# Sliding-window attention and a two-layer block: one transpose for a query block's two blocks of keys

## The chip, the cores and the metric

The kernel runs on one core of a Trainium2 chip. The metric is the device time in microseconds; the kernel before was timed in three runs, and the profile is of one further execution. The engines are TensorE (PE; its weight loads are listed as PEld), VectorE (DVE), ScalarE (ACT), GpSimd (POOL) and SyncE (SP), whose queue issues the loads and stores.

## What is computed

```python
def _attn_ref(q, k, v, n_sink, window):          # q, k, v: 4 x 8 x 768 x 64, n_sink 4, window 128
    scores = np.matmul(q, k.transpose(0, 1, 3, 2)) / np.sqrt(D)
    rel = pos[:, None] - pos[None, :]
    keep = (pos[None, :] < n_sink) | ((rel >= 0) & (rel < window))
    scores = np.where(keep, scores, -1e9)
    a = np.exp(scores - np.max(scores, axis=-1, keepdims=True))
    a = a / (np.sum(a, axis=-1, keepdims=True) + 1e-09)
    return np.matmul(a, v)

x = attn_out.transpose(0, 2, 1, 3).reshape(3072, 512)
h = x @ w_in                                     # 512 x 2048
out = (h * np.cos(h)) @ w_out                    # 2048 x 512
```

## The kernel before

The sequence of a batch is cut into six blocks of 128 rows. A *chunk* is two blocks of queries of one batch (`CB = 2`), so there are 12 chunks of 8 heads each. Since the window is 128 keys, a query block needs its own block of keys (the *diagonal* block), the block before it (*prev*) and the first keys of the batch (the *sinks*, of which 8 columns are carried). A row of probabilities for query block j lies in tile `p` as 264 columns: 128 of prev, 8 sinks, 128 of diag. The first query block of a batch has no prev.

The first three chunks (24 heads, "early") run while the weights are still unpacked; they use a shorter method in plain fp32 (`scores_pe`, `p_out`, `values_pe`). The other nine chunks use splits into two fp32r parts, hi and lo, whose products give nearly fp32: `q_hi`/`q_lo`, `k_hi`/`k_lo`, `v_hi`/`v_lo`, and for the probabilities `p_hi`/`p_lo`. Eight of these nine have a first block that is not block 0 of its batch.

A head of those eight chunks goes through these steps: scores on PE (L885); masking with the row's minimum on DVE (L898); exp with row sums on ACT (L907), four heads together; the reciprocal of the sums on DVE (L916, L917); normalization of each row block on DVE, POOL or ACT (`norm`, L925 and L927, tile `p`); four transposes on PE (`turn`, L997, tile `tp`: prev and diag for each of two query blocks); the fp32r cast of the turned probabilities on ACT (`p_hi`, L1006, tile `phi`) and the remainder on DVE (`p_lo`, L1013, tile `plo`); seven value matmuls on PE (`values`, L1051, tile `av`, with the sinks through `gt` and `vs`); a copy of the lower half on ACT (`x_low`, L1058, tile `xb`) and the sum on DVE (`x_sum`, L1065). `phi` and `plo` have one buffer each. Two heads fill 128 rows of the chunk's x; when eight heads are done the dense layers follow for that chunk in eight slots: `h` (L416), cosine and gate (L425 to L461), `acc` (L476).

Dense work of one chunk stands between the attention steps of the next. What sets the order is a planner (`Plan`): each step has the engines that may take it with an assumed duration, what it waits for, and a priority worked out from the offsets in table `C`. `order()` plays this through and hands out a fixed sequence for each engine, which the engines then follow in order; steps with several engines are placed there too. Steps marked `port=True` on DVE are not planned at the same time as POOL's. 160 filling matmuls (`idle`, L1320) go in at the start where PE would have nothing.

The two transposes for each query block are issued by

```python
c0 = 0 if (kb == i - 1 or i == 0) else o.sw
nc.tensor.transpose(out=o.tp[:, n * P : (n + 1) * P], in_=o.p[:, i - o.i0, c0 : c0 + P], identity=ident)
```

Of the kernel before, what the change touches and what calls it, by code (L numbers as in the profile page):

```python
# [16 lines left out]
P = 128  # L17
# [23 lines left out]
def f32(ap):  # L41
    return ap.bitcast(F32)
# [127 lines left out]
def attn_moe_kernel(ctx, tc, q, k, v, n_sink, window, w_in, w_out, out):  # L170
# [485 lines left out]
    def banded_path():  # L656
# [7 lines left out]
        masks = m0, ma, mb = mk[:, :P], mk[:, P : 3 * P], mk[:, 3 * P :]  # L664
        diag, prev, cols = mb[:, SW:], mb[:, :P], ma[:, :P]
        vs = env.vs = ap.tile([P, H // GQ, GQ, 2, D], F32R, name="vs")
        env.kz = ap.tile([P, 2, NT], F32, name="kz", tag="plo")
        env.warm = ps.tile([P, P], F32, name="warm", tag="b0")

        def masked(m):  # L670
# [20 lines left out]
        for a, (b, i0) in enumerate(chunks):  # L691
            for h in range(H):
                o = Rec()
                o.a, o.b, o.i0, o.h, o.pair, o.odd = a, b, i0, h, h // 2, h % 2
                o.kb0 = max(i0 - 1, 0)
                o.nkb = i0 + CB - o.kb0
                o.sj = [j for j in range(CB) if i0 + j >= 2]
                o.cols = [
                    (kb, [i for i in (kb, kb + 1) if i0 <= i < i0 + CB]) for kb in range(o.kb0, o.kb0 + o.nkb)
                ]  # L700
                o.offs = [sum(len(c[1]) for c in o.cols[:n]) for n in range(len(o.cols) + 1)]
                o.n = o.offs[-1]
                o.sw = P if i0 == 0 else SW
                o.w = [P if i0 + j == 0 else o.sw + P for j in range(CB)]
                o.s_ps = {}
                o.tag = f"{b}_{i0}_{h}"
                heads.append(o)
# [126 lines left out]

        def p_out(o):
            def fn(e):
                o.pt = ap.tile([P, 4 * P], F32, name=f"pt_{o.tag}", tag="phi")
                copy(e, o.pt[:, : o.n * P], o.tp[:, : o.n * P])
            return fn

# [63 lines left out]
        def expo(o, j):  # L904
# [5 lines left out]
                )  # L910
            return fn

        def denom(o):
            def fn(e):
                n = o.nq
                nc.vector.tensor_single_scalar(out=o.st[:, 2, :n], in_=o.st[:, 1, :n], scalar=1.0e-9, op=ALU.add)  # L916
                nc.vector.reciprocal(out=o.st[:, 3, :n], in_=o.st[:, 2, :n])  # L917
            return fn

        def norm(o, j):  # L920
            def fn(e):
                w = o.w[j]
                r = o.lead.st[:, 3, o.nth, j : j + 1]
                if e is nc.scalar:
                    e.activation(out=o.p[:, j, :w], in_=o.p[:, j, :w], func=AF.Copy, scale=r)  # L925
                else:
                    e.tensor_scalar(  # L927
                        out=o.p[:, j, :w], in0=o.p[:, j, :w], scalar1=r, scalar2=1.0, op0=ALU.mult, op1=ALU.mult
                    )
            return fn  # L930
# [59 lines left out]
        def turn(o):  # L990
            def fn(e):
                o.tp = ps.tile([P, 4 * P], F32, name=f"tp_{o.tag}", tag=o.tp_bank)
                n = 0
                for kb, qs in o.cols:
                    for i in qs:
                        c0 = 0 if (kb == i - 1 or i == 0) else o.sw
                        nc.tensor.transpose(  # L997
                            out=o.tp[:, n * P : (n + 1) * P], in_=o.p[:, i - o.i0, c0 : c0 + P], identity=ident
                        )
                        n += 1  # L1000
            return fn

        def p_hi(o):
            def fn(e):
                o.phi = ap.tile([P, 4 * P], F32R, name=f"phi_{o.tag}", tag="phi")
                nc.scalar.copy(out=o.phi[:, : o.n * P], in_=o.tp[:, : o.n * P])  # L1006
            return fn

        def p_lo(o):
            def fn(e):  # L1010
                w = o.n * P
                o.plo = ap.tile([P, 4 * P], F32R, name=f"plo_{o.tag}", tag="plo")
                nc.vector.tensor_tensor(out=o.plo[:, :w], in0=o.tp[:, :w], in1=f32(o.phi)[:, :w], op=ALU.subtract)  # L1013
            return fn

        def values_pe(o, x):
# [179 lines left out]
        def softmax(group):  # L1196
            lead = group[0][1]
            T, DX, NM = (C["TQ"], C["XE"], C["NE"]) if lead.early else (C["T"], C["DX"], C["NM"])
            t = head_time(group[0][0]) - (len(group) - 4) * T - T + 3.9 + DX
            ready = [i for _, o in group for i in o.msk]  # L1200
            ex = [
                add(
                    [("ACT", act(o.w[j]) + 0.19)], expo(o, j), ready, t + 1.02 * n + 0.01 * j, table="exp"
                )
                for n, (_, o) in enumerate(group) for j in range(CB)
            ]
            t += 1.02 * (len(group) - 1) + 0.5
            d = add([("DVE", 0.35)], denom(lead), ex, t)
            for n, (_, o) in enumerate(group):
                o.nm = [  # L1210
                    add(
                        [("POOL", 0.2 + o.w[j] / 1200), ("DVE", dve(o.w[j], True, True)), ("ACT", act(o.w[j]))], norm(o, j), [d],
                        t + NM * n + 0.01 * j, port=True
                    )
                    for j in range(CB)
                ]
                lead.bst.users += o.nm

        def after_softmax(g, o):
# [49 lines left out]
                o.sinks = [o.first.vt, e3]  # L1269
            pt, bhi, blo = buf("tp", 1), buf("phi", 1), buf("plo", 1)  # L1270
            bav = buf("av", 1)
            p0 = add([("PE", 0.107 * o.n)], turn(o), o.nm + [pt], t + DA + 1.3)
            o.bp.users.append(p0)
            p1 = add([("ACT", act(o.n * P, False))], p_hi(o), [p0, bhi], t + DA + 1.8)
            p2 = add([("DVE", dve(o.n * P))], p_lo(o), [p1, blo], t + DA + 2.3)
            pt.users += [p1, p2]
            deps = [p2, v1, bav]
            if o.sj:
                oe = heads[g - o.h % GQ]
                deps += oe.sinks  # L1280
# [251 lines left out]
```

## Time and profile before

| | |
|---|---|
| median of three runs | 752.69 us (750.21 to 754.62) |
| the profiled execution | 750.97 us, its span 749.2 us |
| PE busy | 736.5 us, 98% of the span |
| DVE busy | 625.7 us, 84% |
| ACT busy | 560.7 us, 75% |
| POOL busy | 59.4 us, 8% |
| TensorE clock granted | 0.999 of full speed |

The span runs from the first to the last instruction of the program; the execution's time has 1.8 us more around it. Busy time is the union of an engine's instructions, so overlapping ones count once. Matmuls overlap: a matmul of 256 columns is listed with 0.28 us but the next one starts 0.12 us later, so the step from start to start is what one more or less of them is worth. Idle time of an engine that does not set the end costs nothing. Spans on POOL are rough.

### The profile page before, as it was taken

Reading aid. Unit: us, or ns where it says so; the run is one execution under the profiler, and the core shown is the slowest. Engines: PE = TensorE matmul, PEld = TensorE weight load, DVE = VectorE, ACT = ScalarE, POOL = GpSimd, SP = SyncE. Lnnn points to the kernel's source line nnn. Section 1 sums busy time; section 2 is a strip of 40 time slices with the busy share of each in tenths; the row PEclk is TensorE's granted clock in tenths of the full one; section 3 lists DMA queues with packets and bytes.
Section 4 is the critical chain, followed back from the end, with each engine's and each line's share of the span. In section 5 each row is a group of like instructions: output and inputs, shape, how many; then the busy total and the mean of one; then the engine's idle time right before and its main releaser. Section 6 shows DMA issues by size and latency. Waiting matters only on the chain.

```text
span 749.2 us, 15109 instructions
## 1 busy us (share of the span) xinstructions
PE 736.5 (98%) x4949; PEld 657.3 (88%) x4949; DVE 625.7 (84%) x1698; ACT 560.7 (75%) x1327; POOL 59.4 (8%) x137
## 2 busy tenths in 40 slices
PE   9999999999999999999999999999999999999996
PEld 8787766899899998898999999999999999999995
DVE  6998999768899998989999998998888988865331
ACT  4989778676978878678788688888688788774332
POOL 1000000000101110111110010100011111000000
PEclk9999999999999999999999999999999999999999
DMA  5755575222446546446464433232242333110000
GB/s 156 200 178 180 155 197 144 57 46 40 108 109 160 121 101 154 106 106 188 98 168 120 111 96 61 51 70 41 46 84 47 53 77 59 21 40 7 19 11 32
DMA packets 215608, 71.49 MB, mean 95 GB/s; under 512 B 204256, under 2 KB 204256, under 8 KB 215520
## 3 DMA queue, kind: packets, MB, share of 16 engines
q1 hardware_dynamic: 215232, 70.43, 38.8%
q8 instruction: 41, 0.67, 0.4%
q14 instruction: 47, 0.39, 0.2%
q10 hardware_dynamic: 288, 0.00, 0.0%
HBM read 64.10 MB, written 6.29 MB: 94 GB/s over the span
## 4 chain that ended last, share of the span: by engine, by line
PE 82%; DVE 11%; ACT 3%; DMA 2%; issue 1%; SPq 0%; POOL 0%; DVEq 0%; ACTq 0%; POOLq 0%
PE h L416 33%; PE acc L476 31%; PE av L1051 5%; PE s L885 4%; PE tp L997 4%; PE idle L1320 1%; DVE w_out L530 1%; DVE p L898 1%; DVE w_out L536 1%; PE acc L471 1%; DVE p L927 1%; DVE w_in L530 1%; DVE lo_in L566 1%; PE av L1027 1%; DVE lo_out L566 1%
## 5 line engine op out<-in xcount | busy, mean ns | idle before, releaser
L416 PE MATMUL h<-xhi,hi_in 128*128 128x256 f32 x768 | 222.8, 290 | 1.0 <-ACT pt L404 0.6
L416 PE MATMUL h<-xlo,hi_in 128*128 128x256 f32 x768 | 216.9, 282 | 0.0
L416 PE MATMUL h<-xhi,lo_in 128*128 128x256 f32 x768 | 216.7, 282 | 0.0
L416 PEld LDWEIGHTS h<-xhi,hi_in 128*128 128x128 f32 x768 | 146.1, 190 | 5.1 <-DVE glo L461 1.0
L416 PEld LDWEIGHTS h<-xhi,lo_in 128*128 128x128 f32 x768 | 146.2, 190 | 3.3 <-issue 0.5
L416 PEld LDWEIGHTS h<-xlo,hi_in 128*128 128x128 f32 x768 | 146.1, 190 | 0.0
L476 PE MATMUL acc<-hi_out,ghi 128*128 128x512 f32 x352 | 143.4, 407 | 0.4 <-DVE raw L406 0.4
L476 PE MATMUL acc<-hi_out,glo 128*128 128x512 f32 x352 | 138.4, 393 | 0.0
L476 PE MATMUL acc<-lo_out,ghi 128*128 128x512 f32 x352 | 138.3, 393 | 0.0
L425 ACT ACTIVATE yt<-h 128x512 int32<-128x512 f32 x96 | 57.2, 596 | 59.1 <-PE h L416 56.9
L898 DVE CUSTOM_DVE_ANT_0 p<-s,mk 128x264 f32<-128x264 f32 (+1 forms) x192 | 75.5, 400 | 23.0 <-PE s L885 18.9
L431 DVE SCALAR_TENSOR_TENSOR r<-h,yt 128x512 f32<-128x512 f32 x96 | 65.5, 682 | 34.4 <-ACT yt L425 34.0
L907 ACT ACTIVATE p<-p,st 128x264 f32<-128x264 f32 (+1 forms) x192 | 93.6, 489 | 0.5
L476 PEld LDWEIGHTS acc<-hi_out,glo 128*128 128x128 f32 x352 | 66.1, 188 | 15.0
L438 ACT ACTIVATE r<-r,neg 128x512 f32<-128x512 f32 x96 | 69.1, 723 | 9.7 <-DVE r L431 9.1
L476 PEld LDWEIGHTS acc<-hi_out,ghi 128*128 128x128 f32 x352 | 66.4, 189 | 7.7 <-DVE raw L406 0.6
L476 PEld LDWEIGHTS acc<-lo_out,ghi 128*128 128x128 f32 x352 | 66.6, 189 | 6.6
L461 DVE TENSOR_TENSOR glo<-h,ghi 128x512 fp32r<-128x512 f32 x88 | 60.1, 683 | 10.0 <-ACT ghi L455 9.9
L443 DVE TENSOR_TENSOR h<-h,r 128x512 f32<-128x512 f32 x88 | 60.2, 686 | 2.8 <-ACT r L438 2.7
L455 ACT CAST ghi<-h 128x512 fp32r<-128x512 f32 x88 | 51.3, 583 | 14.9 <-PE acc L476 14.2
L885 PE MATMUL s<-r,l 128*128 128x264 f32 (+2 forms) x288 | 59.3, 286 | 0.4 <-ACT vr L935 0.2
L885 PEld LDWEIGHTS s<-r,l 128*128 128x128 f32 x288 | 48.8, 189 | 7.9 <-DVE st L898 0.9
(128 smaller groups left out, 1328.1 us busy)
## 6 DMA issues: line engine op xcount, KB each, us to landing
raw<-in_moe_w_in_dram SPq DMA_DIRECT2D x32, 512.0 KB
raw<-in_moe_w_out_dram SPq DMA_DIRECT2D x32, 512.0 KB
xk<-in_k_dram SPq DMA_DIRECT2D x256, 48.0 KB
out_dram<-raw SPq DMA_DIRECT2D x24, 256.0 KB
v<-in_v_dram SPq DMA_DIRECT2D x64, 96.0 KB
xq<-in_q_dram SPq DMA_DIRECT2D x144, 32.0 KB
v<-in_v_dram SPq DMA_DIRECT2D x32, 64.0 KB
xq<-in_q_dram SPq DMA_DIRECT2D x24, 64.0 KB
```

Source lines behind the costliest of these rows:

```text
L416: nc.tensor.matmul(out=o.h[:, t, :], lhsT=w[:, fs], rhs=xx[:, c, :], start=(c == 0 and n == 0), stop=(c == NC - 1 and n == 2),)
L425: nc.scalar.activation(out=yt, in_=o.h, func=AF.Copy, scale=INV2PI, bias=0.25)
L431: nc.vector.scalar_tensor_tensor(out=o.r, in0=o.h, scalar=INV2PI, in1=yt, op0=ALU.mult, op1=ALU.subtract)
L438: nc.scalar.activation(out=o.r, in_=o.r, func=AF.Sin, scale=TWOPI_DOWN, bias=quarter)
L443: nc.vector.tensor_tensor(out=o.h, in0=o.h, in1=o.r, op=ALU.mult)
L455: nc.scalar.copy(out=o.ghi, in_=o.h)
L461: e.tensor_tensor(out=o.glo, in0=o.h, in1=f32(o.ghi), op=ALU.subtract)
L476: nc.tensor.matmul(out=x.acc[j], lhsT=gg[:, t, j * P : (j + 1) * P], rhs=w, start=(f == 0 and n == 0), stop=(f == NFT - 1 and n == 2),)
L885: nc.tensor.matmul(out=o.s_ps[j][:, :w], lhsT=o.l[:, j * P : (j + 1) * P], rhs=r.rearrange("p n s -> p (n s)")[:, c0 : c0 + w], start=(n = ...
L898: nc.vector.tensor_tensor_reduce(out=o.p[:, j, :w], in0=o.s_ps[j][:, :w], in1=masks[min(o.i0 + j, 2)][:, :w], op0=ALU.add, op1=ALU.min, sc ...
L907: nc.scalar.activation(out=o.p[:, j, :w], in_=o.p[:, j, :w], func=AF.Exp, bias=o.lead.st[:, 0, o.nth, j : j + 1], scale=-1.0, accum_out=o. ...
L1051: nc.tensor.matmul(out=dst, lhsT=lhs, rhs=rhs, start=(n == 0), stop=(n == len(seq) - 1), skip_group_check=True)
```

## The change

In the eight chunks without a block 0 (64 heads, `o.one`), a row of prev is nonzero only right of the row's own position and a row of diag only up to it, since the window is as long as a block: the two never overlap. After exp, a new step `lap` on DVE or POOL adds the 128 columns of diag onto the 128 of prev, for both query blocks in one instruction of 128x2x128; normalization then covers 136 columns (`o.nw`) instead of 264; `turn` makes two transposes instead of four; `p_hi` and `p_lo` handle 256 columns instead of 512. The two blocks are parted after the turn by two selections on POOL (`part`, `affine_select`), which take hi and lo together (128x4x128 each): the first writes the diag half, the second overwrites the sum with its prev half. `phi` and `plo` become the two halves of one lasting tile `pz` with one buffer, so `p_hi` waits for both to be free. The value matmuls read `pz` as they read `phi` and `plo`. The kz and pt tiles of the early heads share that memory (`firsts`). The numbers of table `C` are new almost throughout.

```diff
+                o.one = i0 > 0
+                o.nw = [SW] * CB if o.one else o.w
...
+        def lap(o):
+            def fn(e):
+                e.tensor_tensor(out=o.p[:, :, :P], in0=o.p[:, :, :P], in1=o.p[:, :, SW:], op=ALU.add)
+            return fn
...
         def norm(o, j):
             def fn(e):
-                w = o.w[j]
+                w = o.nw[j]
...
-                for kb, qs in o.cols:
+                for j in range(CB if o.one else 0):
+                    nc.tensor.transpose(out=o.tp[:, j * P : (j + 1) * P], in_=o.p[:, j, :P], identity=ident)
+                for kb, qs in o.cols if not o.one else ():
...
+                if o.one:
+                    nc.scalar.copy(out=env.pz4[:, 0, :, 0], in_=o.tp[:, :NT].rearrange("p (j r) -> p j r", j=CB))
+                else:
+                    nc.scalar.copy(out=o.phi[:, : o.n * P], in_=o.tp[:, : o.n * P])
...
+                if o.one:
+                    nc.vector.tensor_tensor(
+                        out=env.pz4[:, 1, :, 0], in0=o.tp[:, :NT].rearrange("p (j r) -> p j r", j=CB),
+                        in1=f32(env.pz4)[:, 0, :, 0], op=ALU.subtract,
+                    )
...
+        def part(n):
+            def fn(e):
+                sign = (-1, 1)[n]
+                nc.gpsimd.affine_select(
+                    out=env.pz4[:, :, :, n], in_=f32(env.pz4)[:, :, :, 0], pattern=[[0, 2], [0, CB], [sign, P]],
+                    compare_op=ALU.is_ge, fill=0.0, base=n - 1, channel_multiplier=-sign,
+                )
+            return fn
...
+            laps = [
+                [add(sub(NT), lap(o), ex[CB * n : CB * n + CB], t + 1.02 * n + 0.3 + C["LP"], port=True)] if o.one else []
...
-            p1 = add([("ACT", act(o.n * P, False))], p_hi(o), [p0, bhi], t + DA + 1.8)
-            p2 = add([("DVE", dve(o.n * P))], p_lo(o), [p1, blo], t + DA + 2.3)
+            p1 = add([("ACT", act(n * P, False))], p_hi(o), [p0, bhi, blo], t + DA + 1.8)
+            p2 = add([("DVE", dve(n * P))], p_lo(o), [p1], t + DA + 2.3)
             pt.users += [p1, p2]
-            deps = [p2, v1, bav]
+            if o.one:
+                p1 = add([("POOL", 0.18 + 2 * NT / 1200)], part(1), [p1, p2], t + DA + 2.7)
+                p2 = add([("POOL", 0.18 + 2 * NT / 1200)], part(0), [p1], t + DA + 3.2)
+            deps = [p1, p2, v1, bav]
...
-    "T": 6.142, ...  "DA": 0.079, "DV": 5.203, ...
+    "T": 7.838, ...  "DA": 0.108, "DV": 3.174, ...
```

What the new order makes of this is seen at three places. In the names, `_3_2_3` is batch 3, first block 2, head 3; the last number is the buffer's. First PE, around the values of head 2 and the turn of head 3 in batch 3, before:

```order
L885 MATMUL s_3_2_7_0_8303<-r2_3_2_7_8292,l_3_2_7_8244 128x264
L1051 MATMUL av_3_2_2_8308<-phi_3_2_2_8279,vr_3_2_2_8286 128x256
L1051 MATMUL av_3_2_2_8308<-gt_77,vs_94 128x256
L1051 MATMUL av_3_2_2_8308<-phi_3_2_2_8279,vr_3_2_2_8286 128x128
L1051 MATMUL av_3_2_2_8308<-plo_3_2_2_8299,vr_3_2_2_8286 64x128
L1051 MATMUL av_3_2_2_8308<-plo_3_2_2_8299,vr_3_2_2_8286 64x256
L1051 MATMUL av_3_2_2_8308<-phi_3_2_2_8279,vr_3_2_2_8286 128x128
L1051 MATMUL av_3_2_2_8308<-plo_3_2_2_8299,vr_3_2_2_8286 64x128
L997 MATMUL tp_3_2_3_8319<-ident_76,p_3_2_3_7877 128x128 x4
```

and PE at the same place now:

```order
L1003 MATMUL tp_3_2_3_8261<-ident_76,p_3_2_3_7782 128x128 x2
L416 MATMUL h_75_8226<-xhi_9_7360,hi_in_4_462 128x256
L416 MATMUL h_75_8226<-xhi_9_7360,lo_in_4_503 128x256
L416 MATMUL h_75_8226<-xlo_9_7376,hi_in_4_462 128x256
L416 MATMUL h_75_8226<-xhi_9_7360,hi_in_5_513 128x256
L416 MATMUL h_75_8226<-xhi_9_7360,lo_in_5_527 128x256
L416 MATMUL h_75_8226<-xlo_9_7376,hi_in_5_513 128x256
L1083 MATMUL av_3_2_2_8275<-pz_2099,vr_3_2_2_8188 128x256
```

The turn of the next head, two transposes instead of four, has moved from behind the values of this head to a place ahead of them, with dense work between.

On POOL, in batch 1 while its blocks 2 and 3 are worked on, before (`tk`: sink columns copied into K; `p`: normalization; `vr`: remainder of v):

```order
L406 COPY tk_1_2_5_3741<-ts_1_2_0_3162 128x3x8
L927 TENSOR_SCALAR p_1_2_1_3456<-p_1_2_1_3456,st_1_2_0_3326 128x264
L927 TENSOR_SCALAR p_1_2_2_3550<-p_1_2_2_3550,st_1_2_0_3326 128x264
L940 TENSOR_TENSOR vr_1_2_1_3979<-v32_74,vr_1_2_1_3979 128x3x64
L406 COPY tk_1_2_7_4031<-ts_1_2_0_3162 128x3x8
L940 TENSOR_TENSOR vr_1_2_2_4053<-v32_74,vr_1_2_2_4053 128x3x64
L940 TENSOR_TENSOR vr_1_2_3_4113<-v32_74,vr_1_2_3_4113 128x3x64
```

and POOL there now:

```order
L1042 AFFINE_SELECT pz_2099<-pz_2099 128x4x128 x8
L406 COPY tk_1_2_5_3739<-ts_1_2_0_3160 128x3x8
L935 TENSOR_SCALAR p_1_2_1_3412<-p_1_2_1_3412,st_1_2_0_3313 128x136
L935 TENSOR_SCALAR p_1_2_2_3536<-p_1_2_2_3536,st_1_2_0_3313 128x136
L406 COPY tk_1_2_6_3839<-ts_1_2_0_3160 128x3x8
L1042 AFFINE_SELECT pz_2099<-pz_2099 128x4x128 x8
```

Eight selections stand for four heads; the remainders of v have left POOL here. In the whole program POOL has 128 selections, 38 normalizations (before 55), 6 remainders of v (before 35) and 19 sink copies (before 35). Of the 192 normalizations DVE now has 56 (before 81) and ACT 98 (before 56); of the remainders of v DVE has 66 (before 37).

On DVE, at the end of batch 1, around the remainder of the probabilities of head 3 of its last chunk, before:

```order
L1065 TENSOR_TENSOR x_6_1_4977<-av_1_4_2_4926,xb_75 64x256
L443 TENSOR_TENSOR h_42_4820<-h_42_4820,r_42_4934 128x512
L898 ISA p_1_4_7_4972,st_1_4_4_4623<-s_1_4_7_1_4979,mk_93 128x264
L898 ISA st_1_4_4_4623 128x1
L858 STREAM_TRANSPOSE tk_2_2_0_4999<-xk_73 128x3x128
L1013 TENSOR_TENSOR plo_1_4_3_5003<-tp_1_4_3_4947,phi_1_4_3_4966 128x512
L406 COPY tk_2_2_0_4999<-ts_2_2_0_4955 128x3x8
```

and DVE there now:

```order
L1097 TENSOR_TENSOR x_6_1_5004<-av_1_4_2_4960,xb_75 64x256
L948 TENSOR_TENSOR vr_1_4_3_4994<-v32_74,vr_1_4_3_4994 128x3x64
L879 TENSOR_TENSOR r2_2_2_0_5020<-tk_2_2_0_4968,r1_2_2_0_5002 128x408
L855 TENSOR_TENSOR l_2_2_0_5006<-tq_2_2_0_4990,l_2_2_0_5006 64x256
L1029 TENSOR_TENSOR pz_2099<-tp_1_4_3_4947,pz_2099 128x2x128
L918 TENSOR_TENSOR p_1_4_4_4612<-p_1_4_4_4612 128x2x128
L901 ISA p_2_2_0_5046,st_2_2_0_5047<-s_2_2_0_0_5036,mk_93 128x264
```

The remainder (now 128x2x128) stands behind a remainder of v, which DVE did not have here before, and ahead of the first of the new sums (L918). All 64 sums are on DVE.

## Rows read from the trace of the kernel before

**Rows 1.** The page, part 1: busy us, share of span, instructions.

```profile
PE 736.5 (98%) x4949; PEld 657.3 (88%) x4949; DVE 625.7 (84%) x1698; ACT 560.7 (75%) x1327; POOL 59.4 (8%) x137
```

**Rows 2.** Stretches: from:to, length, then each engine's busy us, clock, DMA.

```profile
0.00:170.00 170.00, 164.39 (x972) 132.30 (x973) 146.42 (x393) 128.88 (x326) 7.09 (x22) 1.00 0.52 145
170.00:690.00 520.00, 518.76 (x3658) 477.52 (x3657) 461.12 (x1279) 414.25 (x973) 52.35 (x116) 1.00 0.39 88
380.00:450.00 70.00, 70.00 (x497) 64.79 (x496) 67.19 (x198) 56.82 (x131) 7.81 (x18) 1.00 0.48 117
```

**Rows 3.** PE's waits: who waited for whom, us in total, times, longest.

```profile
PE warm L240 <- POOL ident L230: 1.4, 1, 1.4
...
PE h L416 <- ACT pt L404: 0.6, 1, 0.6
```

**Rows 4.** Groups by line and shape, PE: busy us, mean ns, idle before.

```profile
L997 PE MATMUL tp<-ident,p 128*128 128x128 f32 x352 | 54.8, 274 | 0.0
```

**Rows 5.** Timeline of PE around one turn: start us, us, instruction.

```profile
307.58 0.62 PE L997 MATMUL tp<-ident,p 128*128 128x128 f32 x4
...
308.27 0.40 PE L476 MATMUL acc<-lo_out,ghi 128*128 128x512 f32 x1
308.51 0.39 PE L476 MATMUL acc<-hi_out,glo 128*128 128x512 f32 x1
```

**Rows 6.** Groups by shape, ACT: the cast removed in part, one of 256.

```profile
L1006 ACT CAST phi<-tp 128x512 fp32r<-128x512 f32 x64 | 37.4, 585 | 1.6 <-PE tp L997 0.2
...
L341 ACT CAST xhi<-x 128x256 fp32r<-128x256 f32 x36 | 14.5, 402 | 2.4 <-DVE x L1065 2.4
```

**Rows 7.** Groups by shape, DVE: what is removed, added and moved.

```profile
L1013 DVE TENSOR_TENSOR plo<-tp,phi 128x512 fp32r<-128x512 f32 x64 | 43.7, 682 | 3.0 <-ACT phi L1006 2.4
...
L927 DVE TENSOR_SCALAR p<-p,st 128x264 f32<-128x264 f32 x50 | 20.8, 465 | 0.2
...
L362 DVE TENSOR_TENSOR xlo<-x,xhi 128x256 fp32r<-128x256 f32 x36 | 14.9, 414 | 1.6 <-ACT xhi L341 1.4
...
L940 DVE TENSOR_TENSOR vr<-v,vr 128x192 fp32r<-128x192 f32 x35 | 12.2, 350 | 0.2
```

**Rows 8.** Groups by shape, POOL: two-input remainders, a copy, the only selection.

```profile
L940 POOL TENSOR_TENSOR vr<-v,vr 128x192 fp32r<-128x192 f32 x29 | 18.0, 622 | 136.3 <-ACT vr L935 126.7 <-DVE glo L461 9.6
L406 POOL COPY tk<-ts 128x24 f32<-128x24 f32 x35 | 7.3, 210 | 122.8 <-DVE r L876 116.7 <-DVE ts L735 6.1
L940 POOL TENSOR_TENSOR vr<-v,vr 128x128 fp32r<-128x128 f32 x6 | 3.0, 508 | 34.2 <-ACT vr L935 28.2 <-DMA xk<-in_k_dram 5.9
...
L230 POOL TENSOR_SCALAR_AFFINE_SELECT ident<-ident 128x128 f32<-128x128 f32 x1 | 0.3, 293 | 0.1
```

**Rows 9.** Line 927, the normalization: shortest/median/longest ns on each engine.

```profile
L927 DVE TENSOR_SCALAR p<-p,st x81: 271/349/593, 27.7 to 664.9; 128x264 f32<-128x264 f32 x50, 128x256 f32<-128x256 f32 x16, 128x128 f32<-128x128 f32 x15
L927 POOL TENSOR_SCALAR p<-p,st x55: 375/520/1041, 25.9 to 664.3; 128x264 f32<-128x264 f32 x47, 128x128 f32<-128x128 f32 x6, 128x256 f32<-128x256 f32 x2
```

**Rows 10.** Timelines of DVE and POOL: normalizations side by side, and one alone.

```profile
260.34 1.86 DVE L927 TENSOR_SCALAR p<-p,st 128x264 f32<-128x264 f32 x4
...
260.48 1.57 POOL L927 TENSOR_SCALAR p<-p,st 128x264 f32<-128x264 f32 x3 [3.75 <-DVE st L917]
...
411.65 0.34 DVE L927 TENSOR_SCALAR p<-p,st 128x264 f32<-128x264 f32 x1
```

**Rows 11.** Timeline of all engines: from one head's values to the next's.

```profile
303.68 0.22 PE L1051 MATMUL av<-plo,vr 128*64 128x128 f32 x1
...
303.99 0.37 ACT L1058 COPY xb<-av 64x256 f32<-64x256 f32 x1 [0.17 <-PE av L1051]
...
304.45 0.59 ACT L1006 CAST phi<-tp 128x512 fp32r<-128x512 f32 x1
...
305.87 0.69 DVE L1013 TENSOR_TENSOR plo<-tp,phi 128x512 fp32r<-128x512 f32 x1
...
306.98 0.28 PE L1051 MATMUL av<-phi,vr 128*128 128x256 f32 x1
```

More of the change, by code (lines that the diff above doesn't have):

```diff
@@ L28 @@
 C = {
[7 rows of a table removed]
[3 rows of a table added]
+    "NWF": 0.232, "PB": 5, "PEN": 29.309, "PL": 3, "POOLF": 4.428, "POOLPEN": -1.361, "QE": 5.937, "R": 2, "RAW": 2,
[3 rows of a table added]
 }
@@ L666, in banded_path @@
         vs = env.vs = ap.tile([P, H // GQ, GQ, 2, D], F32R, name="vs")
-        env.kz = ap.tile([P, 2, NT], F32, name="kz", tag="plo")
+        firsts = ap.tile([P, 2, 4 * P], F32, name="firsts", tag="pz")
+        env.kz = firsts[:, 1].rearrange("p (a n) -> p a n", a=2)
         env.warm = ps.tile([P, P], F32, name="warm", tag="b0")
@@ L836, in fn @@
             def fn(e):
-                o.pt = ap.tile([P, 4 * P], F32, name=f"pt_{o.tag}", tag="phi")
+                o.pt = firsts[:, 0]
                 copy(e, o.pt[:, : o.n * P], o.tp[:, : o.n * P])
@@ L1004, in fn @@
             def fn(e):
-                o.phi = ap.tile([P, 4 * P], F32R, name=f"phi_{o.tag}", tag="phi")
-                nc.scalar.copy(out=o.phi[:, : o.n * P], in_=o.tp[:, : o.n * P])
+                if not hasattr(env, "pz"):
+                    env.pz = ap.tile([P, 2, 4 * P], F32R, name="pz", tag="pz")
+                    env.pz4 = env.pz.rearrange("p a (j n r) -> p a j n r", j=CB, n=2)
+                o.phi, o.plo = env.pz[:, 0], env.pz[:, 1]
+                if o.one:
+                    nc.scalar.copy(out=env.pz4[:, 0, :, 0], in_=o.tp[:, :NT].rearrange("p (j r) -> p j r", j=CB))
+                else:
+                    nc.scalar.copy(out=o.phi[:, : o.n * P], in_=o.tp[:, : o.n * P])
             return fn
@@ L1011, in fn @@
                 w = o.n * P
-                o.plo = ap.tile([P, 4 * P], F32R, name=f"plo_{o.tag}", tag="plo")
-                nc.vector.tensor_tensor(out=o.plo[:, :w], in0=o.tp[:, :w], in1=f32(o.phi)[:, :w], op=ALU.subtract)
+                if o.one:
[3 more added lines that the diff above has]
+                    )
+                else:
+                    nc.vector.tensor_tensor(out=o.plo[:, :w], in0=o.tp[:, :w], in1=f32(o.phi)[:, :w], op=ALU.subtract)
+            return fn
[6 more added lines that the diff above has]
+                )
             return fn
@@ L1206, in softmax @@
             ]
+            laps = [
+                [add(sub(NT), lap(o), ex[CB * n : CB * n + CB], t + 1.02 * n + 0.3 + C["LP"], port=True)] if o.one else []
+                for n, (_, o) in enumerate(group)
+            ]
             t += 1.02 * (len(group) - 1) + 0.5
@@ L1211, in softmax @@
                     add(
-                        [("POOL", 0.2 + o.w[j] / 1200), ("DVE", dve(o.w[j], True, True)), ("ACT", act(o.w[j]))], norm(o, j), [d],
+                        [("POOL", 0.2 + o.nw[j] / 1200), ("DVE", dve(o.nw[j], True, True)), ("ACT", act(o.nw[j]))], norm(o, j), [d, *laps[n]],
                         t + NM * n + 0.01 * j, port=True
@@ L1271, in after_softmax @@
             bav = buf("av", 1)
-            p0 = add([("PE", 0.107 * o.n)], turn(o), o.nm + [pt], t + DA + 1.3)
+            n = CB if o.one else o.n
+            p0 = add([("PE", 0.107 * n)], turn(o), o.nm + [pt], t + DA + 1.3)
             o.bp.users.append(p0)
-            p1 = add([("ACT", act(o.n * P, False))], p_hi(o), [p0, bhi], t + DA + 1.8)
-            p2 = add([("DVE", dve(o.n * P))], p_lo(o), [p1, blo], t + DA + 2.3)
+            p1 = add([("ACT", act(n * P, False))], p_hi(o), [p0, bhi, blo], t + DA + 1.8)
+            p2 = add([("DVE", dve(n * P))], p_lo(o), [p1], t + DA + 2.3)
             pt.users += [p1, p2]
-            deps = [p2, v1, bav]
+            if o.one:
+                p1 = add([("POOL", 0.18 + 2 * NT / 1200)], part(1), [p1, p2], t + DA + 2.7)
+                p2 = add([("POOL", 0.18 + 2 * NT / 1200)], part(0), [p1], t + DA + 3.2)
+            deps = [p1, p2, v1, bav]
             if o.sj:
```

13 rows, old and new, of the table C are left out of this document.

## Prediction

> **What bounds the kernel now.** I read the busy shares of the page first: PE is busy for 736.5 of 749.2 us, DVE for 84%, ACT for 75%, GpSimd (POOL) for 8% [rows 1]. Shares hide stages, so the stretches come next. From 170 to 690 us, where all the heads that this change touches lie, PE is busy for 518.76 of 520 us; DVE for 461.12, which is 88.7%; in its fullest 70 us DVE is busy for 67.19 (96%) and PE still for all 70.00 [rows 2]. PE's own waits have twelve kinds that sum to 6.1 us; the two shown are the first and the fourth of that list [rows 3], and most of PE's idle time lies before 170 us: 5.6 us there, 1.2 us in the stretch behind it [rows 2]. So TensorE work sets the time: a matmul slot taken away is time gained, as long as nobody makes PE wait. DVE is second, some 4 to 11% away.
>
> **What PE loses.** 64 heads (8 chunks whose first query block is not block 0, times 8 heads) now turn two blocks where they turned four: 128 transposes fewer. The price of one: in the timeline a group of four begins at 307.58; the second matmul behind it begins at 308.27 and such a matmul takes 308.51 - 308.27 = 0.24 us, so four transposes held PE for 0.69 - 0.24 = 0.45 us, 0.113 each [rows 5]. From all of them: 96 groups (64 of four, 32 of three), 54.8 us busy, the last of each group counted in full with 0.274, leave (54.8 - 96 x 0.274) / 256 = 0.111 us for a step [rows 4]. 128 x 0.111 = **-14.2 us**, all inside the stretch where PE is full. The value matmuls that follow stay as they are, seven for a head.
>
> **ACT and DVE.** ACT copies 256 columns of a head where it copied 512: 64 x (0.585 - 0.402) = -11.7 us, the second price being another 256-column cast [rows 6]. It takes 42 of the normalizations from the other engines; at no more than 0.40 us each that is +17. With ACT busy for 414 of 520 us [rows 2] a net of some +5 is hidden: 81% busy stays behind PE's work. DVE: the remainder falls from 512 to 256 columns, 64 x (0.682 - 0.414) = -17.2; the new sums are two-input operations over 256 columns, 64 x 0.414 = +26.5; 27 more remainders of v at 0.350 make +9.5, since GpSimd gives them up; normalizations fall from 81 to 56 and most from 264 to 136 columns, 50 x 0.465 - 30 x 0.31 = 14.0 and five others at 0.33, so -15.6 (0.31 for 136 columns is an estimate below the shortest 264-column ones, 0.34) [rows 7, 10]. Net **+3 us on DVE**, which PE's work hides only if DVE keeps its idle time: 464 us in a stretch of 520 - 14.2 = 505.8 are 91.7%. At the 96% that ran without a PE wait it could hold 485.6 us. So DVE has **room for 21.6 us more, 0.17 us for each of the 128 selections**; beyond that every microsecond on DVE is one of the program.
>
> **What GpSimd gets: the unknown price.** The selections read and write 128x512 each; before has one such instruction, 128x128, 0.293 us [rows 8]. A 24-column copy takes 0.21, so at most some 0.1 of the 0.293 is for its columns, and 384 more cost at most 384 x 0.83 ns = 0.32: 0.61 us. The steepest slope on GpSimd in the trace is that of two-input remainders, (0.622 - 0.508) / 64 = 1.8 ns a column, which makes 0.98 us [rows 8]. I take 0.61, since a selection reads one tensor, as the copy does. 128 x 0.61 = 78 us on an engine with 59 us, that gives up about 30: it has the time. For a tight loop the Trainium skill (GPSIMD Engine Reference, section Elementwise, side-by-side cycle accounting) gives 1.8 cycles an element, 0.77 us for 512; an estimate by that page would add 128 x 0.16 = 20 us to GpSimd and nothing to my sum, since it only enters through waits. The row of 0.293 for 128 columns speaks for less.
>
> **The wait that it adds.** Values of a head now wait on PE for the second selection; behind them on PE stands everything else, in order. ACT's cast of the next head needs the one buffer pz free, so the loop runs from values to values. In the trace: last value matmul begins at 303.68, ACT's copy of its lower half at 303.99, the cast at 304.45 until 305.04, the remainder at 305.87 after 0.83 of queueing, until 306.56, values at 306.98 [rows 11]. Now: 0.31 + 0.46 + 0.40 + 0.41 + 2 x 0.61 + 0.1 for handovers = 2.9 us, with that queueing 3.7. Against this stands the work that the order puts between: counted matmul by matmul at the steps of the trace (0.12 us for 256 columns, 0.23 for 512), from the later of turn and previous values to the head's values, the least of the 64 heads has 3.5 us, 14 have under 4.3, the middle one 5.0 (before 2.1 and 4.3). 47 heads are turned ahead of the previous head's values (before 15). So at 0.61 the loop is covered but for one head; GpSimd's other work (sink copies, normalizations) queues behind selections, and K's remainder on DVE waits for the copies, but the order places these a head earlier. New waits in the steady stretch: about 0.
>
> The order of the first 170 us is new as well, loads on the SP queue included; PE is idle there for 5.6 us [rows 2]. That can shrink or double: -2 to +5 us. I charge half of what is idle now, **+2.5**, for start and stray waits together.
>
> **Sum.** 750.97 (this execution; span 749.2 and 1.8 around it) - 14.2 + 2.5 = 739.3. The median of the runs shown lies 1.7 above that execution, so **741.0**.
>
> **Rivals.**
> 1. *The port that DVE and GpSimd share eats most of it.* At 260.34 four normalizations on DVE take 1.86 us beside three on GpSimd; one alone at 411.65 takes 0.34 [rows 10]; the line's spread, 0.271 to 0.593, says the same [rows 9]. So a meeting costs the DVE instruction some 0.24 us. If every selection meets one such operation, DVE gets 128 x 0.24 = 30.7: 494.7 / 0.96 = 515.3 instead of 505.8, 9.5 us lost: 750.5. For it: the sums and the remainders of K, q and v, some four a head, read two SBUF tensors. Against: the planner keeps such steps apart from GpSimd's in its own time, and some 27 meetings of normalizations go. The Trainium skill (SBUF: State Buffer, section Who interferes with whom) states that rule: a DVE instruction with two SBUF inputs, or in a two-port mode, and a GpSimd instruction that reads SBUF exclude each other for their whole length; the rows agree for the normalizations.
> 2. *Selections run slower than 0.61, with few meetings.* At 0.87 (between the two slopes) the loop needs 2.9 + 0.52 + 0.83 = 4.25, and only those 14 heads wait, up to 0.5 us: 745.
> 3. *Slower than before.* Selections as long as the longest normalization on GpSimd, 1.04 us [rows 9], and three in five meet a DVE operation that waits half of that: 0.31 each, 40 us, (464 + 40) / 0.96 = 525: 19 us more than the forecast, 760. It turns into a loss from 0.26 us a selection: (21.6 + 14.2 - 2.5) / 128.
> 4. *The gain is there, the new start loses it in part*: 5 us more idle before 170 us, 746. The change cannot fail to remove its transposes; they are counted in the order.
>
> **How the numbers follow.** Forecast 0.60 (own range 737 to 745), rival 1 0.17, rival 2 0.10, rival 3 0.07, rival 4 0.06. A measurement can tell about 0.5%, 3.8 us: faster is under 748.9, slower over 756.5. Faster: forecast, 2, 4 and a little of 1, 0.79; the same: the rest of 1 and some of 3, 0.13; slower 0.08. The range runs from 736 (all 14.2 and 2 from the start, less 0.5) to 751, which takes in rival 1.
>
> **What would show it.** Right: PE busy near 722 us, the transposes' group at 224 instructions and some 40 us, PE still full from 170 us on, selections near 0.6 us and no wait of value matmuls on GpSimd in PE's list. Rival 1 shows as DVE above 96% with its two-input groups' means up by 0.1 to 0.2 us; rival 2 as "values wait for the selection" in PE's list; rival 4 as waits before 170 us. I would be wrong if a selection took over 0.9 us, or if DVE, not PE, had no idle left.

## The result and the profile after

The changed kernel takes 743.84 us (median of four runs, 743.45 to 744.67), the kernel before 752.6 beside it: a ratio of 0.9886 (95% interval 0.9856 to 0.9917). That is 8.8 us less, where 11.6 were forecast: faster by the prediction's own measure (under 748.9), inside the range, 2.8 us from the predicted time. The profiled execution took 743.69 us, its span 742.0, 7.2 less than before; before's profiled execution, 750.97, lay 1.6 below its median.

The page's part 1 of the changed kernel (busy us, share of the span, instructions), against [rows 1]:

```profile
PE 724.5 (98%) x4821; PEld 643.0 (87%) x4821; DVE 626.0 (84%) x1765; ACT 558.0 (75%) x1386; POOL 112.9 (15%) x203
```

PE has 128 instructions fewer and 12.0 us less busy time, DVE is where it was (+0.3), ACT 2.7 lower, GpSimd 53.5 higher. The groups that answer to [rows 4, 6 to 8] (busy us, mean ns, idle before and what ended it) show what was traded:

```profile
L1003 PE MATMUL tp<-ident,p 128*128 128x128 f32 x128 | 24.5, 272 | 0.2 <-DVE pz L1029 0.2
L1007 PE MATMUL tp<-ident,p 128*128 128x128 f32 x96 | 16.3, 277 | 0.8 <-ACT p L933 0.7
L1020 ACT CAST pz<-tp 128x256 fp32r<-128x256 f32 x64 | 23.8, 371 | 1.8 <-PE tp L1003 0.6
L1029 DVE TENSOR_TENSOR pz<-tp,pz 128x256 fp32r<-128x256 f32 x64 | 26.6, 416 | 0.4 <-ACT pz L1020 0.3
L918 DVE TENSOR_TENSOR p<-p 128x256 f32<-128x256 f32 x64 | 25.1, 406 | 3.4 <-ACT p L910 3.3
L948 DVE TENSOR_TENSOR vr<-v,vr 128x192 fp32r<-128x192 f32 x62 | 21.7, 350 | 0.8
L1042 POOL TENSOR_SCALAR_AFFINE_SELECT pz<-pz 128x512 fp32r<-128x512 f32 x128 | 85.4, 667 | 265.8 <-DVE pz L1029 220.6
```

The transposes hold PE for 24.5 + 16.3 = 40.8 us where they held 54.8 [rows 4]. But PE isn't as full as it was. The stretches of the changed kernel (from:to, length, busy us of PE, PEld, DVE, ACT, POOL, clock, DMA share, GB/s), against [rows 2]:

```profile
0.00:170.00 170.00, 161.92 (x952) 129.21 (x953) 148.17 (x392) 125.81 (x326) 3.97 (x15) 1.00 0.52 145
170.00:676.00 506.00, 502.64 (x3509) 460.46 (x3508) 454.40 (x1336) 410.77 (x1024) 106.36 (x184) 1.00 0.40 90
...
380.00:450.00 70.00, 67.80 (x471) 61.38 (x470) 66.50 (x203) 57.67 (x145) 15.72 (x27) 1.00 0.50 118
```

Before 170 us PE idles for 8.1 us (5.6 before), behind it for 3.4 of 506 (1.2 of 520 before), and the stretch of 70 us that had no gap now has 2.2. PE's waits (for whom, us in total, times, longest), against [rows 3]:

```profile
PE h L416 <- ACT firsts L404: 1.6, 1, 1.6
...
PE h L416 <- DVE glo L461: 0.9, 2, 0.5
PE h L416 <- DVE xlo L362: 0.8, 1, 0.8
...
PE s L888 <- DVE r L879: 0.5, 1, 0.5
PE gp L987 <- DVE gc L977: 0.5, 1, 0.5
```

No matmul waits for a selection. Shown idle time is less than PE's loss, since the listed ends of matmuls reach over short gaps. So I priced every matmul at the median step from start to start of its kind (same tiles, same shape): PE's work falls from 727.3 to 712.6 us, by 14.7, and what the span has beyond this work, its *rest*, rises from 21.9 to 29.4, by 7.5. These are two executions; by the medians of the runs the loss is 14.7 - 8.8 = 5.9. The question for the experiments is what made these 6 to 7 us: the selections, the sums, or the order itself.

### The profile page after: what moved, and what is told of

Its sections match the earlier page's. It is cut to its first block, busy times and chain, and to the rows that moved or that the text cites. A ratio compares the mean times of both kernels' runs of the same rounds, so it can differ in the third digit from the quotient of the medians.

```text
span 742.0 us, 15106 instructions
## 1 busy us (share of the span) xinstructions
PE 724.5 (98%) x4821; PEld 643.0 (87%) x4821; DVE 626.0 (84%) x1765; ACT 558.0 (75%) x1386; POOL 112.9 (15%) x203
## 4 chain that ended last, share of the span: by engine, by line
PE 75%; DVE 11%; ACT 8%; DMA 2%; issue 2%; SPq 1%; DVEq 0%; ACTq 0%
PE h L416 32%; PE acc L476 29%; PE av L1083 5%; PE s L888 4%; PE tp L1003 2%; ACT p L910 2%; ACT p L933 1%; DMA xq<-in_q_dram 1%; DVE p L901 1%; DMA raw<-in_moe_w_in_dram 1%; DVE w_out L530 1%; PE acc L471 1%; DVE r L431 1%; DVE w_out L536 1%; DVE lo_in L566 1%
## 5 line engine op out<-in xcount | busy, mean ns | idle before, releaser
L416 PE MATMUL h<-xhi,hi_in 128*128 128x256 f32 x768 | 225.9, 294 | 3.0 <-ACT firsts L404 1.6
L1042 POOL TENSOR_SCALAR_AFFINE_SELECT pz<-pz 128x512 fp32r<-128x512 f32 x128 | 85.4, 667 | 265.8 <-DVE pz L1029 220.6
L901 DVE CUSTOM_DVE_ANT_0 p<-s,mk 128x264 f32<-128x264 f32 (+1 forms) x192 | 75.3, 399 | 25.2 <-PE s L888 21.9
L455 ACT CAST ghi<-h 128x512 fp32r<-128x512 f32 x88 | 51.3, 583 | 14.2 <-PE acc L476 13.3
```

The source lines that it names most:

```text
L416: nc.tensor.matmul(out=o.h[:, t, :], lhsT=w[:, fs], rhs=xx[:, c, :], start=(c == 0 and n == 0), stop=(c == NC - 1 and n == 2),)
L455: nc.scalar.copy(out=o.ghi, in_=o.h)
L901: nc.vector.tensor_tensor_reduce(out=o.p[:, j, :w], in0=o.s_ps[j][:, :w], in1=masks[min(o.i0 + j, 2)][:, :w], op0=ALU.add, op1=ALU.min, sc ...
L1042: nc.gpsimd.affine_select(out=env.pz4[:, :, :, n], in_=f32(env.pz4)[:, :, :, 0], pattern=[[0, 2], [0, CB], [sign, P]], compare_op=ALU.is_g ...
```

## Experiments

Three theories stood at the start. *Sums*: the 64 new instructions on DVE make what PE waits for late. *Selections*: they lengthen DVE's instructions or the loop through the one buffer `pz`. *Order*: the new table of offsets makes an order that leaves PE more gaps, whatever the steps cost. A table also settles which engine takes a step, so "order" stands for both here; no run separates them. The times of "before" in a set of runs are those beside which its kernels ran, 752.6 to 754.2 us.

### The steps and the table apart

`e1_old_offsets` is the changed kernel with before's table (the new offset `LP` keeps its value), `e2_before_new_offsets` the kernel before with the changed one's. Of e1:

```diff
-    ... "DA": 0.108, ... "DV": 3.174, ... "LP": -0.072, ... "T": 7.838, ...
+    ... "DA": 0.079, ... "DV": 5.203, ... "LP": -0.072, ... "T": 6.142, ...
```

> The new steps (sum, two transposes, two selections) with the table of offsets of before, and the new offset LP at its new value. Three theories on where 7.4 of the 14.6 us of TensorE work went: A, the sums, 0.41 us each on DVE, stand in DVE's queue ahead of what TensorE waits for (xlo, glo, K's remainder); B, the selections, by the port or by the loop over pz; C, the new offsets, which changed the order of the first 170 us and of the rest. A and B expect this run near 744 (742 to 749), since the steps are the same; C expects it below 741, since the order of before lost less. If the old offsets suit the new steps badly, it comes out above 749, which says that the new offsets were needed.

> The kernel before, with the new table of offsets alone: four transposes, no sums, no selections. A and B expect 752.6 within 2 us, the loss needs the new steps. C expects 756 to 761: the offsets cost 4 to 7 us by themselves, half of it before 170 us.

e1 takes 765.87 us, ratio 1.0164 (1.0141 to 1.0188): 1.6% slower than before and 2.8% (21 us) slower than with its own table. e2 takes 757.21, 1.0049 (1.0032 to 1.0067): before's steps lose some 4 us by the new table. Its longest wait on PE, for sink columns, ends at 206 us, and behind it the granted clock is below 1.00 for a while (the wait's row, and a stretch with columns as above):

```profile
PE gp L979 <- DVE gc L969: 3.2, 1, 3.2
```

```profile
205.00:210.00 5.00, 3.60 (x21) 3.37 (x22) 5.00 (x15) 1.93 (x4) 0.00 (x0) 0.79 0.40 141
```

Stretches of e1, columns as above, and PE's waits in 240 to 280 us:

```profile
250.00:255.00 5.00, 4.37 (x31) 3.69 (x30) 4.22 (x12) 4.72 (x18) 1.77 (x3) 1.00 0.61 99
255.00:260.00 5.00, 3.31 (x26) 2.85 (x24) 4.90 (x17) 4.92 (x11) 0.79 (x2) 1.00 0.46 132
260.00:265.00 5.00, 2.32 (x9) 1.46 (x10) 4.86 (x19) 2.92 (x8) 1.31 (x3) 0.63 0.28 46
265.00:270.00 5.00, 3.01 (x14) 2.30 (x14) 4.71 (x15) 1.93 (x5) 2.14 (x3) 0.50 0.58 114
...
280.00:285.00 5.00, 5.00 (x19) 3.94 (x19) 2.23 (x9) 2.17 (x8) 0.23 (x1) 0.82 0.79 210
```

```profile
PE s L888 <- DVE st L901: 3.7, 4, 1.6
PE av L1083 <- POOL pz L1042: 1.9, 2, 1.3
PE tp L1003 <- DVE p L935: 1.3, 1, 1.3
```

DVE is full there (4.90 of 5 us), PE waits for its masks, for selections and for a normalization, and after PE's gaps the granted clock falls from 1.00 to 0.50, 1.2 GHz, until some 282 us. So the steps are worth nothing in an order that is not made for them, and part of e1's loss is the clock, not the waits alone: by its mean over the run, 0.984 beside 0.998, an estimated 11 us of 764 at most. The table is therefore a part of the change with a size of its own, in both directions.

### Without the selections, without the sums

`e3_no_select` and `e5_no_lap` keep the order and drop one new step each; e3 clears `pz` once instead.

```diff
+                    nc.gpsimd.memset(f32(env.pz), 0.0)
...
-                nc.gpsimd.affine_select(
-                    out=env.pz4[:, :, :, n], ...
-                )
```

```diff
-                e.tensor_tensor(out=o.p[:, :, :P], in0=o.p[:, :, :P], in1=o.p[:, :, SW:], op=ALU.add)
+                pass
```

> The selections are left out: pz is cleared once on GpSimd, the value matmuls read its second half as it was cleared, so the values are wrong. The order of all other instructions is that of the new kernel. B expects 738 to 740 (the 5 us that TensorE lost behind 170 us come back). A and C expect 743 to 744.5, since in the trace the selections make nobody long wait: their shortest is 0.637 us, 13 of 128 are over 0.1 us longer.

> The sums are left out (the diagonal block's probabilities are missing): 64 DVE operations of 0.41 us, 0.33 from start to start, some 21 us less on DVE, the order of all else as in the new kernel. A expects 738.5 to 740.5: most of the 5 us lost behind 170 us return. B and C expect 743 to 744.5.

e3 takes 743.85 us (0.988, 0.9854 to 0.9906), e5 743.94 (0.9875, 0.9852 to 0.9897): the time of the changed kernel, both. The stretch from 170 us, of e3:

```profile
170.00:676.00 506.00, 502.82 (x3509) 460.83 (x3509) 451.78 (x1336) 410.93 (x1025) 25.28 (x61) 1.00 0.41 90
```

and of e5:

```profile
170.00:676.00 506.00, 502.94 (x3509) 460.78 (x3509) 437.40 (x1275) 410.76 (x1025) 105.15 (x185) 1.00 0.41 90
```

GpSimd loses 81 us and DVE 17 us in this stretch, and PE's busy time stays within 0.3 us of 502.64; the spans, 741.3 and 741.5, are under 0.8 us shorter than 742.0. Both theories of a costly new step fall, one by one: neither selections nor sums cost more than that at the place where the order has them. No run leaves out both together, and the one buffer `pz` is in all of them; but ACT's 64 casts into it were never kept idle by a value matmul, only once, for 0.6 us, by a turn. What is left is the order.

### How much cover the new steps have

That a step costs nothing doesn't say how far its cover reaches. `e8_three_selects` issues the last selection twice, `e9_four_selects` three times (the same values again), `e10_two_sums` the sum twice, `e7_four_turns` each transpose twice. Of e8 (e9 has `1 + 2 * n`):

```diff
-                nc.gpsimd.affine_select(
+                for _ in range(1 + n):
+                  nc.gpsimd.affine_select(
```

> The last selection of each head is issued twice, three in all: 0.585 us more in the loop over pz and 64 x 0.585 = 37 us more on the port. In the trace of the new kernel the last selection ends 0.05 to 4.6 us before the value matmuls begin, the middle one 0.95. The loop theory expects the heads with less than 0.585 to wait, 13 of 64, in sum 2 us: 746 (744 to 748). The port theory (every selection blocks one DVE operation) expects 64 x 0.24 = 15 us on DVE and 746 to 752 with DVE's two-input groups longer. If neither counts: 744.

> The last selection is issued three times, four in all: 1.17 us more in the loop. By the same margins 46 of 64 heads wait, in sum 19 us: 763 (757 to 770). If the engines' queues have slack that absorbs a late head, less: under 752. If the port counts, more than 770.

> The new kernel with its sum issued twice for each head (the diagonal block counts twice, the values are wrong): 64 x 0.33 = 21 us more on DVE, which the prediction gave 21.6 us of room. Leaving the sums out changed nothing, so if DVE has that room, 744 to 747; if DVE is at its limit as soon as it gets more work, up to 21 us more: over 755.

> Each of the two transposes of a head is issued twice, the second time into a part of the bank that nobody reads: 128 transposes put back, the order of all else as in the new kernel. If the time is TensorE's work, 128 x 0.111 = 14.2 us come back: 758 (756 to 760). If the new kernel is held by DVE or by its order instead, part of it is hidden: under 752.

| | us | ratio to before | DVE busy, us | PE waits for selections, us |
|---|---|---|---|---|
| changed kernel | 743.84 | 0.9886 (0.9856 to 0.9917) | 626.0 | none |
| e8, one more | 752.49 | 0.9983 (0.997 to 0.9996) | 636.2 | 3.4, 10 times |
| e9, two more | 780.25 | 1.0345 (1.0328 to 1.0362) | 647.0 | 23.9, 42 times |
| e10, sums twice | 759.02 | 1.0075 (1.0051 to 1.01) | 652.3 | none |
| e7, transposes twice | 755.62 | 1.0019 (1.0009 to 1.0029) | 626.7 | none |

The loop theory's figures for e8 and e9 were too low, by 6 and 17 us, and the port theory's were met within 0.5 us (746 to 752, over 770); e10 came out over 755, the branch in which DVE has no room, not at 744 to 747. The expectations also took 0.585 us for a selection, where one more adds (156.6 - 112.9) / 64 = 0.68 to GpSimd. The page's part 1 of e8, of e3 and of e10:

```profile
PE 729.9 (97%) x4821; PEld 642.1 (86%) x4821; DVE 636.2 (85%) x1765; ACT 558.5 (74%) x1386; POOL 156.6 (21%) x267
```

```profile
PE 724.5 (98%) x4821; PEld 643.3 (87%) x4821; DVE 623.2 (84%) x1765; ACT 557.8 (75%) x1386; POOL 29.2 (4%) x76
```

```profile
PE 730.9 (97%) x4821; PEld 643.4 (85%) x4821; DVE 652.3 (86%) x1829; ACT 560.9 (74%) x1386; POOL 113.6 (15%) x203
```

All but e10 have the same 1765 instructions on DVE. Its busy time rises by instructions made longer: the sum of their durations goes from 723.8 to 735.0 us in e8. The 128 planned selections cost DVE 626.0 - 623.2 = 2.8 us, 0.02 each. The 64 that e8 adds, of which the order knows nothing, cost it 10.2 us, 0.16 each: rival 1's price was 0.24 for a meeting. The mechanism of rival 1 is there. The planner has a rule of not placing `port` steps beside GpSimd's, which an unplanned selection breaks; that this rule keeps the cost away in the changed kernel is likely, but no run goes without it. The direct wait of e8 is smaller, 3.4 us:

```profile
PE av L1084 <- POOL pz L1043: 3.4, 10, 0.6
```

One selection more than the order planned for makes the weight loads of 22 heads late (by up to 1.1 us) and the matmuls of 10; two more make those of 54 and 42 of the 64 heads late. In the changed kernel the last selection ends 0.05 to 4.6 us before its value matmuls begin, with a median of 0.95: most heads have cover for one selection, few for two. How e8's and e9's losses divide between late heads and longer DVE instructions, these runs do not tell.

e10's 64 further sums add 26.3 us to DVE and 14 to the time (0.0189 of 752.6), though e5 showed that taking them away gives nothing. PE's waits of e10:

```profile
PE h L416 <- DVE glo L461: 4.4, 7, 1.1
PE s L888 <- DVE r L879: 3.3, 6, 0.9
...
PE s L888 <- DVE st L901: 1.1, 2, 0.8
PE gp L988 <- DVE gc L978: 1.0, 1, 1.0
```

DVE is busy for 469.49 of 506 us in its stretch, 92.8%:

```profile
170.00:676.00 506.00, 493.45 (x3398) 446.05 (x3397) 469.49 (x1367) 403.80 (x1006) 103.75 (x178) 1.00 0.40 90
```

DVE's idle time is not a common store from which work can be paid: the steps that PE waits for, `glo` and K's remainder `r`, stand behind sums in DVE's queue and come late though DVE is idle elsewhere.

e7 is the control: 128 transposes more (some 14 us of PE's work) cost 10 us by the ratios, where 14.2 were expected, so time does follow PE's work, and some of the gaps take up work that comes at the right place. e7 says one thing more. With as much work on PE as before, the new steps in the new order end only 1.4 us (0.7 to 2.2) over the kernel before. So, by the ratios, most of the 6 us is not time that the new order adds to any work: it is work taken off PE that this order does not turn into time. The profiled executions put more on the order: the rest of e7 is 26.3 us, 4.4 above before's 21.9.

### Other orders

If the loss is in the order, another order of the same steps should give some of it back. `e6_early_offsets` took before's offsets for the early stage alone, since 2.5 us of the loss are there. `c1_new_table` and `c2_new_table` have tables found by a random search over the offsets, judged by the planner's own play of the order; `e11_before_searched` is the kernel before with a table searched for it in the same way. Of c1 (its line numbers are 8 lower than the changed kernel's):

```diff
-    ... "DA": 0.108, ... "DV": 3.174, "DX": 4.249, ... "LEAD": 0.258, ... "T": 7.838, ... "XE": 2.85, ...
+    ... 'DA': -1.19, ... 'DV': 1.582, 'DX': 2.661, ... 'LEAD': 10.378, ... 'T': 6.808, ... 'XE': 1.123, ...
```

> The new kernel with the offsets of before for the early stage alone (early heads and the unpacking of the weights: E, TE, TQ, QE, XE, AE, S0, WI, WO, WS, WS2, LEAD). After the first four runs the theory is that the new order of the first 170 us loses 2.3 us of TensorE time against the order of before. It expects 741.5 (740 to 743). Its rival, that the start costs the same with either set and the loss comes with the shared steps, expects 743 to 745. Above 746 would mean that the new late offsets need the new early ones.

> The new kernel with a third table of offsets, found by changing the offsets of the new table at random and keeping what lets the planner place TensorE's steps with less between them; steps, durations and latencies that the planner assumes are as they were. If the 22 us that TensorE stands idle in the new kernel (before: 15) are put there by the order, some 6 to 10 us less idle: 735 to 739. If the order is already as good as the engines allow, or the real engines do not follow such an order, 743 or more.

> As c1, another table from a separate series of changes. The order theory expects 736 to 741, its rival 743 or more.

> The steps of the kernel before, with a table of offsets found in the same way and with about the same effort as c1_new_table's. It tells whether the 4 us that the new table gave to the changed kernel are a gain of the steps (they leave an order that the first table of the change did not reach) or of any new table. If before's order was already near what its steps allow: 749 to 753 us, ratio 0.995 to 1.0, and the steps are worth some 13 us when both tables are chosen alike. If a new table gives as much to before as to the changed kernel: 745 to 748, ratio about 0.99, and the steps' worth stays near 8 us.

e6 takes 747.78 us (0.9915, 0.9898 to 0.9931), no better than the changed kernel, where 741.5 was expected: PE is busy for 159.72 of the first 170 us instead of 161.92. The early offsets do not help by themselves, without the rest of their table. c1 takes 740.03 (0.9826, 0.9801 to 0.9851), faster than both kernels, though not the 735 to 739 that the order theory expected; c2 takes 742.23 (0.985, 0.9826 to 0.9874), between the theory's 736 to 741 and its rival's 743, and its interval overlaps that of the changed kernel. Stretches of c1:

```profile
0.00:170.00 170.00, 162.41 (x962) 129.90 (x963) 144.69 (x381) 125.54 (x322) 8.31 (x21) 1.00 0.53 143
170.00:676.00 506.00, 504.90 (x3533) 464.92 (x3532) 459.70 (x1331) 408.82 (x1010) 131.06 (x234) 1.00 0.41 91
...
380.00:450.00 70.00, 70.00 (x491) 64.40 (x491) 66.55 (x197) 54.53 (x133) 23.50 (x43) 1.00 0.49 112
```

PE is full in 380 to 450 us again and idles for 1.1 us in the 506 instead of 3.4. DVE has no less work there (459.70 beside 454.40) and GpSimd has more: the same steps, in another order and in part on other engines, without the gaps. Priced as above, c1's rest is 23.1 us, beside 29.4 of the changed kernel and 21.9 before; behind 170 us, where the changed kernel lost some 5 us against before, c1 loses nothing (4.8 beyond PE's work, 9.9 in the changed kernel, 5.0 before). That profiled execution of c1, 738.09, is its fastest.

e11 takes 751.25 (0.9967, 0.9951 to 0.9983): a new table gives the kernel before 0.3%, the changed one 0.6% (0.9826 / 0.9886 = 0.994). With tables chosen alike the steps are worth 0.9826 / 0.9967 = 0.986, 10.7 us of 752.6, with the two intervals taken together some 8.5 to 12.9; I had expected 13. That is 1.9 more than the two given kernels show, less than the noise of the pair, so it is not shown that before's table was nearer to what its steps allow. Why the best orders found still give 10.7 of some 14.7 us is open: no run here tells an order that the search didn't find from a limit of the steps.

## Why the prediction was right, point by point

- **PE sets the time; 128 transposes are -14.2 us.** Right. The group's rows say 54.8 - 40.8 = 14.0, the price by steps 14.7; "224 transposes with some 40 us" was 40.8. PE busy is 724.5, forecast near 722.
- **ACT hidden, DVE +3.** The conclusion holds, the sizes less: ACT fell by 2.7 us instead of rising by 5, DVE rose by 0.3, and its new sums cost 0.406 each for 0.414. (DVE took 29 more remainders of v, by the counts of the order, not 27: +10.1 for +9.5.)
- **DVE's room of 21.6 us.** This step was wrong as an argument. It took 96% of a stretch as what DVE could carry anywhere. e10 added 26.3 us, 4.7 above that room, and paid 14, with DVE at 92.8% of the stretch, still under the 96%. It did no harm because DVE's work hardly changed; rivals 1 and 3 were priced by the same rule and stand on no better ground.
- **A selection at 0.61 us.** Nearly right. The changed kernel's group by duration (minimum, median, maximum in ns; first and last start):

```profile
L1042 POOL TENSOR_SCALAR_AFFINE_SELECT pz<-pz x128: 637/639/1131, 176.7 to 681.7; 128x512 fp32r<-128x512 f32 x128
```

  The median is 0.639. An estimate by the Trainium skill (GPSIMD Engine Reference, section Elementwise, side-by-side cycle accounting), from its 1.8 cycles an element for a tight loop, was 0.77; the measurement decides. The lower slope in [rows 8] was the right one to take, but 0.61 was no upper bound: the slope is 0.9 ns a column, not 0.83. The upper one, 1.8 ns, was read from means that hold a few disturbed instructions; by the medians of the two shapes in the same trace, 0.602 and 0.464 us, it is 2.2.
- **The loop from values to values, 2.9 us and 3.7 with queueing, covered but for one head.** Right. The timeline of the changed kernel (start us, us, instruction; the bracket is idle time and what ended it) shows it:

```profile
301.77 0.28 PE L1083 MATMUL av<-pz,vr 128*128 128x256 f32 x1
...
302.56 0.37 ACT L1090 COPY xb<-av 64x256 f32<-64x256 f32 x1 [1.16 <-PE av L1083]
303.21 0.37 ACT L1020 CAST pz<-tp 128x256 fp32r<-128x256 f32 x1
304.79 0.41 DVE L1029 TENSOR_TENSOR pz<-tp,pz 128x256 fp32r<-128x256 f32 x1
305.36 1.35 POOL L1042 TENSOR_SCALAR_AFFINE_SELECT pz<-pz 128x512 fp32r<-128x512 f32 x2 [4.74 <-DVE pz L1029]
```

  Two selections take 1.35 us (1.22 forecast). Between cast and remainder 1.2 us pass in DVE's queue here; from the cast's start to the last selection's end it is 2.89 us in the median of the 64 heads, 2.25 at least. My terms for that part, with 0.83 of queueing, were 0.40 + 0.83 + 0.41 + 1.22 = 2.9. No value matmul waits for GpSimd, one weight load does, for 0.3 us.
- **Start and stray waits +2.5 us.** This is the term that was mis-sized: 7.5 were lost by the profiled executions, 5.9 by the medians. I looked for new waits at the new steps and charged all else with half of the old start. The start took 2.5 us by itself, and about 5 came behind it at places that the diff doesn't touch, among them `h` waiting for `xlo` (0.8) and `glo` (0.9), the sink columns, K's remainder. "PE still full from 170 us on" was wrong by that. For the execution the forecast was 739.3 and the result 743.69, 4.4 more: 5.0 from this term, less 0.5 from the transposes. That the median missed by 2.8 only is luck: the 1.7 us between before's execution and its median went into the forecast, and the changed kernel's median lies 0.15 above its execution. One of these places in the timeline of the changed kernel, DVE at 410 us:

```profile
409.43 0.58 DVE L861 STREAM_TRANSPOSE tk<-xk 128x384 f32<-128x384 f32 x1
...
409.93 0.67 DVE L443 TENSOR_TENSOR h<-h,r 128x512 f32<-128x512 f32 x1
...
410.23 0.28 PE L416 MATMUL h<-xhi,lo_in 128*128 128x256 f32 x1
...
410.51 0.23 DVE L973 CAST gc<-p 128x16 fp32r<-128x16 f32 x2
410.70 0.26 DVE L977 TENSOR_TENSOR gc<-p,gc 128x16 f32<-128x16 f32 x2
410.88 0.42 DVE L362 TENSOR_TENSOR xlo<-x,xhi 128x256 fp32r<-128x256 f32 x1
```

  PE reaches the products of `xlo` at 410.35 (0.12 behind the start of the one before), when DVE still has three older steps to finish ahead of it, none of them new; `xlo` is done at 411.30.
- **Rival 1 (the port)** has the right mechanism and a place here: `xlo` on DVE takes 0.780 at most in the changed kernel and 0.427 without selections (e3, the second row):

```profile
L362 DVE TENSOR_TENSOR xlo<-x,xhi x36: 372/416/780, 188.9 to 685.6; 128x256 fp32r<-128x256 f32 x36
L362 DVE TENSOR_TENSOR xlo<-x,xhi x36: 372/416/427, 188.8 to 684.9; 128x256 fp32r<-128x256 f32 x36
```

  In sum it costs DVE 2.8 us and, by e3, the program nothing that can be measured. The Trainium skill (SBUF: State Buffer, section Who interferes with whom) gives the rule that a DVE instruction with two SBUF inputs and a GpSimd instruction that reads SBUF exclude each other; e8 and e9, where DVE's same instructions take 10 and 21 us more, agree, and so does the remainder of the probabilities, which reads PSUM and one SBUF tensor and takes 0.425 at most in the changed kernel and 0.426 with two selections more (e9). **Rivals 2 and 3** did not come: selections are fast and one head's weight load alone waits for them. (In rival 2 the longest wait would have been 4.25 - 3.5 = 0.75 us, not 0.5.) **Rival 4** was half of it: a loss in the order, 2.5 us of it in the start and more behind it.

## What to carry to other kernels

When a change comes with a new order, price the order as a term of its own, and wide: here 6 to 7 of 14 us saved on PE did not reach the time, at places that the diff doesn't name, and before's table with the new steps made a loss of 12. Work taken off the engine that sets the time need not come back in full: in one and the same order 128 transposes were worth 10 us, not 14 (e7). Idle time of the second engine is no budget: taking 17 us off covered steps gave nothing and adding 26 cost 14, so measure the cover at the step (a median of 0.95 us here) before relying on it. To judge new steps, choose the table for both kernels with the same effort; the pair c1 and e11 gives 10.7 us where the two given kernels gave 8.8, a difference within the noise.

## What the hardware showed

A selection of 128x512 on GpSimd takes 0.639 us beside 0.293 for 128x128 [rows 8]: (0.639 - 0.293) / 384 = 0.9 ns a column, under half the slope of the two-input remainders (2.2 ns by their medians). It slows DVE hardly at all where it is planned around (0.02 us each) and by 0.16 us where it is not. And gaps on PE can cost more than themselves: in e1 the granted clock fell to 0.50 at some 261 us, after PE had been busy for 4.37 and 3.31 of 5 us, stayed there until some 282 us, and the mean over the whole run fell to 0.984 (0.998 in the changed kernel).
